# Moving the score maxima and the v maxima between partitions by DMA in a hash-masked attention kernel, with reshaped casts and a new hand-written order

## The chip, the cores and the metric

The kernel runs on one core of a Trainium2 chip. The metric is the device time of one execution in microseconds (us), as the median of several runs. TensorE (PE) multiplies matrices, VectorE (DVE), ScalarE (ACT) and GpSimd (POOL) work on tiles, and SyncE (SP) issues the DMAs of this kernel.

## The reference

Three stages follow each other: an attention whose mask comes from hash buckets, and two feed-forward layers. Cut to what matters:

```python
q_bits = (einsum('bhsd,dk->bhsk', q, proj) > 0)      # 6 bits for each query, the same for keys
mask = q_bucket[:, :, :, None] == k_bucket[:, :, None, :]
scores = where(mask, scale * q @ k.T, -1e9)          # B, H, S, D = 2, 8, 768, 64
attn = exp(scores - scores.max(-1)); attn = attn / (attn.sum(-1) + 1e-9)
x = (attn @ v) as [1536, 512]
h = x @ w_in;  g = P(h) / (Q(h) + 1e-6);  x = g @ w_out     # 512 -> 2048 -> 512
h = x @ w_in2; g = h - tanh(h);           out = g @ w_out2
```

## The kernel before, in words

The attention works on 16 heads, one after another in a software pipeline. Each head has 768 queries and 768 keys, cut into six blocks of 128 (`j`). For a head, in this order:

- `load_qk` loads k and q as one tile with 128 partitions, `split_hi` (ACT) and `split_lo` (POOL) make a rounded part and a rest, and `place` copies them by six DMAs into the operands `TAk`, `TAq`, `TBk`, `TBq`.
- `bits` makes the hash bits with six matmuls. Its out part (DVE) writes them into rows 64 to 107 of `TBk`, and a DMA takes the rows of q into `TBq`.
- `smax` (L456) multiplies a block of 128 queries, taken as weights, by all keys, and DVE takes the maximum of each query over the keys (L460). That is one number in each partition, six columns to a head (`mx`).
- `put_max`, `put_half` (L471 to L477) bring these maxima into row 76 of `TBq`: TensorE transposes `mx` into PSUM (`mt`), DVE negates and bounds it (`mr`), a DMA copies it into the row. There it takes part in the second matmul of `scores`.
- `scores` (L582) makes the transposed scores of a block of keys, ACT takes the exponential (L585). `round_e` rounds it to 16 bits (`eh`), a part on ACT (L591) and the rest on DVE (L593), split by `EH_ACT`; `rest_e` makes the rest `el` on POOL (L602), in the last head partly on DVE (L600).
- `attend` (L634 to L637) multiplies blocks of `eh` and `el` as weights by v in two halves, 18 matmuls of 64 or 65 columns for each `j`; `normalize` divides (DVE).

For each pair of heads v is loaded, and a scale, the same for all partitions, is found from the largest absolute value of each head. `vmax` (L499, DVE) takes a maximum in each partition; `vall` transposes it on TensorE (L508); the `vback` part (L512, L513, DVE) reduces it; the `vagain` part (L516, TensorE) spreads it over the partitions by two small matmuls; `vscale` (L526 to L529, DVE) makes the scale `vsc`. `vhi` (L548, ACT) and `vlo` (L557, DVE; for heads 0 and 1 ACT and POOL) split v into two 16-bit halves, `vmean_of` (L564) adds up v by matmuls. `mt`, `vt` and `vm` share one PSUM bank, the pool `sgl` with one buffer. `fill` (L615) issues matmuls whose result nobody reads. From head 9 on, weights of the first layer are prepared as well (L173 on ACT, L187 and L192 on DVE, L199 on ACT, L200 on POOL). At the end of the attention four blocks of the first layer (`hr`) are woven in with the last head.

The order on every engine is written out by hand: each step has a place in units of one `j`, six to a head, in the tables `T`, `EARLY`, `T_LAST`, and `on(place, step)` sorts them. Engines run their instructions in that order. SP too takes its DMAs in order. The two layers have places in a second table, corrected by `NUDGE`.

Of the kernel before, what the change touches and what calls it, by code (L numbers as in the profile page):

```python
# [10 lines left out]
F32, F32R, F16, I32 = DT.float32, DT.float32r, DT.float16, DT.int32  # L11
# [22 lines left out]
M = dict(a=1, b=3.35, c=3.69, d=5, e=5, y=1.59, scale=3.71, join=3.82, halves=6.35)  # L34
# [10 lines left out]
T = dict(load=-21.57, hi=-15.42, lo=-15.12, place=-14.05, place_a=-12.96, bits=-13.55, bits_out=-12.65,  # L45
         put=-3.12, put_out=-3.08, vhi=-8.38, vlo=-3.99, vmean=-1.97, vmean_out=-0.81, lead=9.98, max=0.3,
         exp=0.42, round=0.9, rest=1.38, pv=(5.37, 6.95, 7.8, 8.75, 8.44, 9.16), pv_last=(5.41, 6.77, 8.07,
         9.01, 8.75, 8.94), norm=9.81, x=14.6, x_out=15.27, v=-16.72, vmax=-11.72, vall=-10.45, vscale=-9.9,
         h0=0.72, slot=0.93, a=0.84, b=1.9, c=2.24, d=4.03, e=4.17, gates=24.8, vback=-10.25, vagain=-9.92,
         w_load=6.0, wt=(-41.29, -22.72, -17.84, -12.24, -8.26, -4.0, 0.32, 3.85), ls=1.0)  # L50
EARLY = {0: dict(load=-61.69, hi=-62.14, lo=-60.39, place=-60.58, bits=-58.96, bits_out=-57.68, place_a=-58.4,
                lead=52.54, put=-46.37, v=-63.23, vmax=-58.62, vall=-56.52, vscale=-54.29, vhi=-6.88,
                vlo=-6.75, vmean=-5.12, vmean_out=-2.89, vback=-56.49, vagain=-55.68, put_half=-47.77,
                ls=0.86),
         1: dict(load=-67.13, hi=-65.44, lo=-65.19, place=-64.04, bits=-59.08, bits_out=-58.81, place_a=-57.52,
                lead=54.94, ls=1.12),
         2: dict(load=-64.89, hi=-61.91, lo=-61.61, place=-61.57, place_a=-61.53, bits=-58.68, bits_out=-58.14,
                lead=9.66, v=-20.61, ls=1.03),
         3: dict(load=-22.52, hi=-15.52, lo=-14.68, place=-14.44, place_a=-13.73, bits=-12.32, bits_out=-11.43,
                lead=9.64)}  # L60
NE = 1
T_LAST = dict(norm=9.87, x=10.11, x_out=10.68)
# [17 lines left out]
 'x_lo 1 1 1': 7.93,  # L80
# [5 lines left out]
 't_sum 1 5 0 3': -0.73}  # L86
# [36 lines left out]
def tile_fn(ctx: ExitStack, tc: tile.TileContext, kq, v, proj, w1i, w1o, a_, b_, w2i, w2o, out):  # L123
# [197 lines left out]
    with ExitStack() as actx:  # L321
# [5 lines left out]

        def single(name):
            return sgl.tile([P, 512], F32, name=name, tag="s")
# [121 lines left out]
        def smax(h, j):  # L451
            if j == 0:
                mx[h] = ap.tile([P, NK], F32, name=f"mx{h}", tag="mx", bufs=4)
            ps = double(f"sm{h}_{j}")[:, :, 0:SH]
            for n in range(2):
                nc.tensor.matmul(ps[:, n], TBq[h][0:76, j * P:(j + 1) * P],  # L456
                                 TBk[h][0:76, n * SH:(n + 1) * SH], start=True, stop=True)

            def out():
                d = nc.vector.tensor_reduce(mx[h][:, j:j + 1], ps, axis=AX.XY, op=ALU.max)  # L460
                if j == NK - 1:
                    sent.setdefault("max", d.ins)

            outs["max", (h, j)] = out
# [37 lines left out]
        nc.vector.memset(pj, 1.0)  # L502
        ones2 = pj[0:2]

        def vall(pr):

            ps = single(f"vt{pr}")
            nc.tensor.transpose(ps[0:2, 0:P], vmx.pop(pr), ident)  # L508

            def back():  # L510
                m = ps[0:2, P + 8:P + 9]
                nc.vector.tensor_reduce(m, ps[0:2, 0:P], axis=AX.X, op=ALU.max)  # L512
                nc.vector.tensor_mul(dg, ident[0:2, 0:2], m.to_broadcast([2, 2]))  # L513

            def again():
                nc.tensor.matmul(ps[:, P:P + 2], ones2, dg, start=True, stop=True)  # L516
                vmx[pr] = ps[:, P:P + 2]

            dg = ap.tile([2, 2], F32, name=f"vdg{pr}", tag="vdg", bufs=2)
            outs["vback", pr], outs["vagain", pr] = back, again  # L520

        def vscale(pr):

            x = vmx.pop(pr)
            xi = x.bitcast(I32)
# [19 lines left out]
        EPS = 1024.0 * 1e-9  # L545
# [14 lines left out]
        def vmean_of(h):  # L560
            ps = single(f"vm{h}")[:, 0:D]
# [5 lines left out]
            def out():  # L567
                t, c = VM[h % 3], 2.0 ** 14 * EPS / S
# [18 lines left out]
        def round_e(h, j):  # L587
            eh[h, j] = ap.tile([P, S], F16, name=f"eh{h}_{j}", tag="eh", bufs=6)
            n = (EH_ACT if h < BH - 1 else EH_ACT_LAST)[j]
            if n:  # L590
                nc.scalar.copy(eh[h, j][:, 0:n], ef[h, j][:, 0:n])  # L591
            if n < S:
                nc.vector.tensor_copy(eh[h, j][:, n:S], ef[h, j][:, n:S])  # L593

        def rest_e(h, j):
            el[h, j] = ap.tile([P, S], F16, name=f"el{h}_{j}", tag="el", bufs=6)
            n = (EL_DVE if h < BH - 1 else EL_DVE_LAST)[j]
            e = ef.pop((h, j))
# [8 lines left out]
        def fill(n):  # L607

            if not warm:
                warm.append(pvp.tile([P, 512], F32, name=f"pvw{len(pv)}", tag="pv"))  # L610
                new = True
            else:
                new = False
            for x in range(n):
                nc.tensor.matmul(warm[0][:, NK * PW:512], ones16, ones16[:, 0:512 - NK * PW], start=new and x == 0,  # L615
                                 stop=False, skip_group_check=True)

        def attend(h, j):
# [13 lines left out]
            for t in range(NK):  # L632
                q = slice(t * P, (t + 1) * P)
                nc.tensor.matmul(out(t), a[:, q], vb[:, j, 0:PW], start=False, stop=False, skip_group_check=True)  # L634
                nc.tensor.matmul(out(t)[:, 0:D], a[:, q], vb[:, j, PW:PW + D], start=False, stop=False,  # L635
# [56 lines left out]
        for h in range(BH):  # L692
# [30 lines left out]
            if h % 2 == 0:  # L723
# [5 lines left out]
                on(g + T["vscale"], vscale, h // 2)  # L729
# [18 lines left out]
        on(TT["gates"] + 2, out_of, "gates", 0)  # L748
        for _, _, fn, args in sorted(tasks, key=lambda x: x[:2]):
            fn(*args)  # L750

# [428 lines left out]
```

## Time and profile before

| | |
|---|---|
| median of 3 runs | 766.49 us (766.38 to 767.56) |
| the profiled execution's own time | 770.33 us |
| its span, first to last instruction | 768.5 us |
| attention, to the first large matmul of the layers | 0 to 260 us of the span |
| first layer, second layer | 260 to about 503, about 503 to 764 us |
| TensorE busy | 740.6 us (96% of the span) |

Times of rows are microseconds from the start of the span. A busy TensorE is not TensorE at its peak, since matmuls overlap: the start of one to the start of the next is its real price. [...]

### The profile page before, as it was taken

The numbers are of one execution on the slowest core, as the hardware profiler recorded it, in microseconds if no ns is written. First come the engines' busy times: TensorE is split into PE (matmuls) and PEld (weight loads), VectorE is DVE, ScalarE is ACT, GpSimd is POOL, SyncE is SP. The second block draws the span as 40 slices with busy tenths as digits, with TensorE's granted clock in tenths as the row PEclk, the third lists the DMA queues.
The fourth block names the chain that finished last, engine by engine and source line by source line (L and its number), as shares of the span: only waits on it lengthen the run. The fifth ranks groups of instructions, "written<-read, shape, count | busy, mean of one in ns | idle before, by whom it ended". The sixth has DMA issues, their size and how long they took to land.

```text
span 768.5 us, 13965 instructions
## 1 busy us (share of the span) xinstructions
PE 740.6 (96%) x5273; PEld 639.6 (83%) x5273; DVE 625.3 (81%) x988; ACT 492.6 (64%) x831; POOL 556.4 (72%) x458
## 2 busy tenths in 40 slices
PE   5999999999998899999999999999999999999997
PEld 3888888888786788888888888887989899989886
DVE  6688999999988888879899998999656766767655
ACT  2577888878896788776666677767554354344421
POOL 3498999898998687787777789968555465465621
PEclk9699999999999999999999999999999999999999
DMA  7573546537421231121121212201031220311003
GB/s 195 147 181 108 146 130 166 158 93 191 119 85 55 71 95 56 55 82 56 57 81 56 82 29 64 73 1 56 27 110 41 70 82 28 110 55 55 28 28 137
DMA packets 41051, 66.52 MB, mean 87 GB/s; under 512 B 3844, under 2 KB 27492, under 8 KB 40984
## 3 DMA queue, kind: packets, MB, share of 16 engines
q1 hardware_dynamic: 40984, 65.63, 29.4%
q8 instruction: 41, 0.67, 0.4%
q14 instruction: 26, 0.21, 0.1%
HBM read 43.00 MB, written 3.15 MB: 60 GB/s over the span
## 4 chain that ended last, share of the span: by engine, by line
PE 77%; DVE 12%; POOL 4%; issue 2%; ACT 2%; DMA 1%; SPq 0%; ACTq 0%; DVEq 0%; POOLq 0%
PE y L1005 17%; PE y L784 12%; PE h L262 12%; PE st L582 7%; PE h2b L922 6%; PE h2e L922 4%; PE h2a L922 4%; PE sm L456 3%; DVE mx L460 3%; PE bits L431 2%; PE hr L262 2%; PE pv L634 1%; PE pv L635 1%; DVE eh L593 1%; PE pv L637 1%
## 5 line engine op out<-in xcount | busy, mean ns | idle before, releaser
L602 POOL TENSOR_TENSOR el<-e,eh 128x768 f16<-128x768 f32 (+1 forms) x95 | 158.8, 1687 | 26.1 <-ACT eh L591 15.1
L1005 PE MATMUL y<-wO,G 128*128 128x512 f32 x576 | 145.1, 393 | 0.3 <-POOL G L990 0.3
L990 POOL TENSOR_TENSOR G<-tmp,G 128x384 fp32r<-128x384 f32 x64 | 66.1, 1034 | 95.6 <-ACT G L985 85.6
L1005 PEld LDWEIGHTS y<-wO,G 128*128 128x128 f32 x576 | 107.0, 188 | 19.1 <-POOL G L990 0.8
L585 ACT ACTIVATE e<-st,lnk 128x768 f32<-128x768 f32 x96 | 86.2, 899 | 29.8 <-PE st L582 26.6
L460 DVE TENSOR_REDUCE mx<-sm 128x1 f32<-128x768 f32 x96 | 90.2, 951 | 9.6 <-PE sm L456 8.4
L1020 DVE TENSOR_TENSOR ya<-y,ya 128x512 f32<-128x512 f32 x84 | 58.1, 692 | 34.5 <-PE y L1005 34.5
L318 POOL TENSOR_TENSOR G<-vec,G 128x512 fp32r<-128x512 f32 x44 | 57.1, 1304 | 26.1 <-ACT G L313 26.0
L591 ACT CAST eh<-e 128x768 f16<-128x768 f32 (+2 forms) x93 | 65.8, 708 | 1.9
L784 PE MATMUL y<-G,wO 128*128 128x512 f32 x288 | 66.7, 389 | 0.0
L784 PE MATMUL y<-G,wE 128*128 128x512 f32 x288 | 66.3, 389 | 0.0
L262 PE MATMUL h<-x,wO 128*128 128x512 f32 x288 | 66.3, 389 | 0.0
L582 PE MATMUL st<-TA 128*128 128x384 f32 x192 | 57.5, 381 | 6.3 <-DVE wt L192 3.3
L784 PEld LDWEIGHTS y<-G,wE 128*128 128x128 f32 x288 | 54.1, 188 | 11.2
L262 PEld LDWEIGHTS h<-x,wO 128*128 128x128 f32 x288 | 54.1, 188 | 11.2
L784 PEld LDWEIGHTS y<-G,wO 128*128 128x128 f32 x288 | 54.0, 188 | 11.1
L634 PEld LDWEIGHTS <-eh 128*128 128x128 f16 x576 | 53.4, 97 | 9.2 <-issue 8.7
L634 PE MATMUL pv<-VB,eh 128*128 128x65 f16 x540 | 59.5, 195 | 0.0
L635 PE MATMUL pv<-VB,eh 128*128 128x64 f16 x540 | 59.1, 196 | 0.0
L637 PE MATMUL pv<-VB,el 128*128 128x65 f16 x540 | 58.6, 193 | 0.4 <-POOL el L602 0.4
L922 PE MATMUL h2b<-x,wE 128*128 128x384 f32 x288 | 58.1, 336 | 0.6 <-DVE tmp L938 0.6
L456 PE MATMUL sm<-TBk,TBq 76*128 76x384 f32 x192 | 54.7, 372 | 3.4 <-DVE mx L460 2.0
(170 smaller groups left out, 1877.4 us busy)
## 6 DMA issues: line engine op xcount, KB each, us to landing
raw<-in_w1i_dram SPq DMA_DIRECT2D x16, 512.0 KB
raw<-in_w1o_dram SPq DMA_DIRECT2D x16, 512.0 KB
raw<-in_w2i_dram SPq DMA_DIRECT2D x16, 512.0 KB
raw<-in_w2o_dram SPq DMA_DIRECT2D x16, 512.0 KB
kq<-in_kq_dram SPq DMA_DIRECT2D x16, 384.0 KB
TA<-A SPq DMA_DIRECT2D x32, 192.0 KB
TA<-Bl SPq DMA_DIRECT2D x32, 192.0 KB
vraw<-in_v_dram SPq DMA_DIRECT2D x8, 384.0 KB
```

Of the source, the lines that this page charges most:

```text
L262: nc.tensor.matmul(ps, l[:, dc], r, start=(n == 0), stop=(n == 11))
L456: nc.tensor.matmul(ps[:, n], TBq[h][0:76, j * P:(j + 1) * P], TBk[h][0:76, n * SH:(n + 1) * SH], start=True, stop=True)
L460: d = nc.vector.tensor_reduce(mx[h][:, j:j + 1], ps, axis=AX.XY, op=ALU.max)
L582: nc.tensor.matmul(ps[:, n], l[h][0:k, j * P:(j + 1) * P], q[h][0:k, n * SH:(n + 1) * SH], start=(k == P), stop=(k < P))
L585: outs["e", (h, j)] = lambda: nc.scalar.activation(halved(e), ps, AF.Exp, scale=1.0 / math.sqrt(D), bias=lnk)
L602: nc.gpsimd.tensor_sub(el[h, j][:, n:S], e[:, n:S], eh[h, j][:, n:S])
L634: nc.tensor.matmul(out(t), a[:, q], vb[:, j, 0:PW], start=False, stop=False, skip_group_check=True)
L635: nc.tensor.matmul(out(t)[:, 0:D], a[:, q], vb[:, j, PW:PW + D], start=False, stop=False, skip_group_check=True)
L637: nc.tensor.matmul(out(t), l[:, q], vb[:, j, 0:PW], start=False, stop=(j == NK - 1), skip_group_check=True)
L784: nc.tensor.matmul(ps, l[:, o], r, start=(n == 0), stop=(n == 11))
L922: nc.tensor.matmul(banks[n, k], w_in(j, l)[:, o:o + P], x[:, r, dt], start=new and z == 0, stop=z == 5, skip_group_check=not new)
L1005: nc.tensor.matmul(ps, g[:, l, o], r, start=(z == 0), stop=(z == 5))
```

## The change

Score maxima: block `j` of `smax` now takes every sixth query, `6 p + j`, as its 128 weights. So partition `p` holds six neighbouring queries, DVE negates and bounds `mx` where it lies, and one DMA from 128 partitions (24 bytes each) writes row 76. The transpose goes. v maxima: a DMA brings `vmx` into one partition, DVE reduces it and makes the scale there, a second DMA spreads the scale over 128 partitions; the transposes, the small matmuls and `vscale` go. Casts: the DVE part of `eh` has 3 or 5 rows of 128 (before, 256 or 640 columns in one run), in rows of 130 places. `vlo`: ACT writes the scaled v into PSUM, DVE subtracts from there. One PSUM bank, `sbank`, is kept for the sums of v, the scaled v and the scale. In `vback` three more instructions, those of `vscale`, run on the one partition. Fillers, places and nudges are new; a `fill` that opens a new PSUM tile after the first `vmean_of` issues a quarter as many matmuls of 512 columns. A program `before` looks over the order while the kernel is built; it adds no instruction.

```diff
-EH_ACT = (768, 768, 128, 768, 512, 768)
+EH_ACT = (384, 768, 128, 768, 384, 768)
+EP = P + 2
-EH_ACT_LAST = (0, 0, 768, 0, 640, 768)
-EL_DVE_LAST = (128, 0, 0, 128, 128, 768)
-FILL = ((1.54, 30), (100.1, 16), (200, 50))
+EH_ACT_LAST = (128, 0, 768, 384, 768, 768)
+EL_DVE_LAST = (640, 0, 0, 640, 640, 768)
+FILL = ((100.1, 31), (199.95, 71), (-62.62, 25), (-57.32, 46), (-1.76, 12), (91.54, 25))
...
         def smax(h, j):
-                nc.tensor.matmul(ps[:, n], TBq[h][0:76, j * P:(j + 1) * P],
+                nc.tensor.matmul(ps[:, n], TBq[h][0:76].rearrange("k (p t) -> k t p", p=P)[:, j],
                                  TBk[h][0:76, n * SH:(n + 1) * SH], start=True, stop=True)
...
         def put_part(h, m, t0, n):
-            ps = single(f"mt{h}_{t0}")[0:n, 0:P]
-            nc.tensor.transpose(ps, m[:, t0:t0 + n], ident)
+            mr = ap.tile([P, n], F32R, name=f"mr{h}_{t0}", tag="mr", bufs=2)
...
+            nc.vector.tensor_scalar(mr, m, -1.0, -LOWEST, op0=ALU.mult, op1=ALU.min)
             def out():
-                mr = ap.tile([n, P], F32R, name=f"mr{h}_{t0}", tag="mr", bufs=2)
-                nc.vector.tensor_scalar(mr, ps, -1.0, -LOWEST, op0=ALU.mult, op1=ALU.min)
-                nc.sync.dma_start(TBq[h][76:77, t0 * P:(t0 + n) * P].bitcast(F32), mr.bitcast(F32))
+                row = TBq[h][76:77].bitcast(F32).rearrange("o (p t) -> o p t", p=P)
+                src = mr.bitcast(F32)
+                nc.sync.dma_start(row[:, :, t0:t0 + n], src if n < NK else src.rearrange("p a b -> p (a b)"))
...
         def vall(pr):
-            ps = single(f"vt{pr}")
-            nc.tensor.transpose(ps[0:2, 0:P], vmx.pop(pr), ident)
+            row = ap.tile([1, 2 * P], F32, name=f"vrow{pr}", tag="vrow", bufs=2)
+            nc.sync.dma_start(row.rearrange("o (p h) -> o p h", h=2), vmx.pop(pr))
+            sc = ap.tile([1, 2], F32, name=f"vs1{pr}", tag="vs1", bufs=2)
             def back():
-                m = ps[0:2, P + 8:P + 9]
-                nc.vector.tensor_reduce(m, ps[0:2, 0:P], axis=AX.X, op=ALU.max)
-                nc.vector.tensor_mul(dg, ident[0:2, 0:2], m.to_broadcast([2, 2]))
+                o = SH + D + 2 * (pr % 2)
+                x = sbank[0:1, o:o + 2]
+                nc.vector.tensor_reduce(x, row.rearrange("o (p h) -> o h p", h=2), axis=AX.X, op=ALU.max)
...
             def again():
-                nc.tensor.matmul(ps[:, P:P + 2], ones2, dg, start=True, stop=True)
+                vs = ap.tile([P, 2], F32, name=f"vsc{pr}", tag="vsc", bufs=3)
+                nc.sync.dma_start(vs, sc.unsqueeze(1).to_broadcast([1, P, 2]))
...
         def vlo(h):
-            nc.vector.scalar_tensor_tensor(out=t[:, :, D + 1:2 * D + 1], in0=vsl(h), scalar=vsc[h],
-                                           in1=t[:, :, 0:D], op0=ALU.mult, op1=ALU.subtract)
+            x = sbank[:, 0:SH].rearrange("p (t d) -> p t d", t=NK)
+            nc.scalar.activation(x, vsl(h), AF.Copy, scale=vsc[h])
+            nc.vector.tensor_sub(t[:, :, D + 1:2 * D + 1], x, t[:, :, 0:D])
...
         def round_e(h, j):
-            eh[h, j] = ap.tile([P, S], F16, name=f"eh{h}_{j}", tag="eh", bufs=6)
+            t = ap.tile([P, NK * EP], F16, name=f"eh{h}_{j}", tag="eh", bufs=6)
+            w = P if n == S else EP
+            t = eh[h, j] = t[:, 0:NK * w].rearrange("p (t w) -> p t w", w=w)[:, :, 0:P]
+            r, e = n // P, ef[h, j].rearrange("p (t w) -> p t w", w=P)
...
         def fill(n):
...
+            if new and VM_SET:
+                w = VB[0][:, 0:4, 0:P]
+                for x in range(n // 4):
+                    nc.tensor.matmul(warm[0].rearrange("p (a b) -> p a b", a=4), ones16, w, start=x == 0, stop=False,
+                                     skip_group_check=True)
+                return
```

Of the places, those of the steps that move data between partitions are, before and after: `put` -3.12 and -3.09, `vmax` -11.72 and -12.75, `vall` -10.45 and -12.36, `vback` -10.25 and -10.26, `vagain` -9.92 and -9.9, `vhi` -8.38 and -7.56, `vlo` -3.99 and -4.8, `place` -14.05 and -13.78, `bits_out` -12.65 and -12.91. In the first pair `vall` and `vback` stand together at -56.59.

## Rows read from the trace of the kernel before

**Rows 1.** Busy time of each engine, granted clock and DMA: two heads, then the layers' joint.

```profile
79.09:91.55 12.46, 12.46 (x173) 11.39 (x173) 11.34 (x22) 10.64 (x18) 11.20 (x7) 1.00 0.47 117
...
157.50:171.98 14.48, 13.42 (x179) 11.71 (x176) 14.08 (x24) 10.20 (x16) 13.08 (x9) 1.00 0.45 114
...
500.00:510.00 10.00, 8.57 (x43) 7.47 (x43) 9.62 (x19) 5.74 (x12) 3.91 (x4) 1.00 0.01 2
```

**Rows 2.** The chain that ended last, in order of time: start, duration, what.

```profile
26.75 2.72 PE st L582 x8
29.48 2.88 PE pvw L615 x30
...
79.09 1.12 PE bits L431 x6
...
143.29 1.11 PE bits L431 x6
...
238.65 3.63 PE hr L262 x12
```

**Rows 3.** Groups of VectorE by shape, 40 to 240 us: busy, mean ns, idle before.

```profile
L593 DVE CAST eh<-e 128x256 f16<-128x256 f32 x14 | 18.7, 1338 | 0.1
...
L557 DVE SCALAR_TENSOR_TENSOR VB<-vraw,vsc,VB 128x384 f16<-128x384 f32 x14 | 12.8, 916 | 0.2
L593 DVE CAST eh<-e 128x640 f16<-128x640 f32 x14 | 12.4, 889 | 1.0 <-ACT e L585 1.0
L651 DVE TENSOR_TENSOR xt<-pv,rz 128x384 f32<-128x384 f32 x14 | 7.8, 557 | 0.5
```

**Rows 4.** VectorE in order of time, at 92 us.

```profile
92.24 1.83 DVE L593 CAST eh<-e 128x256 f16<-128x256 f32 x1
```

**Rows 5.** GpSimd in order of time, at 90 us.

```profile
90.64 3.28 POOL L602 TENSOR_TENSOR el<-e,eh 128x768 f16<-128x768 f32 x2
```

**Rows 6.** Stretches at the start and the end of the attention, columns as in rows 1.

```profile
20.00:32.00 12.00, 11.70 (x64) 9.89 (x63) 8.04 (x12) 4.43 (x7) 1.64 (x1) 0.50 0.78 202
...
235.00:238.40 3.40, 2.95 (x31) 2.61 (x32) 3.30 (x8) 2.61 (x4) 3.40 (x3) 0.77 0.44 154
```

**Rows 7.** TensorE in order of time, 86 to 95 us.

```profile
86.26 0.51 PE L456 MATMUL sm<-TBk,TBq 76*128 76x384 f32 x2
...
87.00 0.20 PE L634 MATMUL pv<-VB,eh 128*128 128x65 f16 x1
...
88.13 0.27 PE L471 MATMUL mt<-ident,mx 128*6 128x128 f32 x1
...
88.59 0.52 PE L582 MATMUL st<-TBq,TBk 77*128 77x384 f32 x2
88.94 0.52 PE L456 MATMUL sm<-TBk,TBq 76*128 76x384 f32 x2
...
94.88 0.52 PE L582 MATMUL st<-TBq,TBk 77*128 77x384 f32 x2
```

**Rows 8.** Single lines: ns least, median and most; first and last start; shapes.

```profile
L499 DVE TENSOR_REDUCE vm<-vraw x8: 947/953/955, 6.6 to 189.9; 128x2 f32<-128x768 f32 x8
...
L508 PEld LDWEIGHTS vt<-ident,vm x8: 80/82/122, 7.7 to 191.1; 128*2 128x2 f32 x8
...
L456 PEld LDWEIGHTS sm<-TBk,TBq x192: 186/189/338, 13.1 to 218.4; 76*128 76x128 f32 x192
```

**Rows 9.** Groups of ScalarE by shape, 40 to 240 us, columns as in rows 3.

```profile
L591 ACT CAST eh<-e 128x768 f16<-128x768 f32 x59 | 48.9, 828 | 1.3
...
L591 ACT CAST eh<-e 128x512 f16<-128x512 f32 x14 | 8.7, 619 | 0.4
L548 ACT ACTIVATE VB<-vraw,vsc 128x384 f16<-128x384 f32 x13 | 8.0, 615 | 0.0
```

**Rows 10.** SP's DMA issues in order of time, at 89 us.

```profile
89.20 0.78 SPq L477 DMA_DIRECT2D TBq<-mr  x1
```

**Rows 11.** The chain at 176 us, a DMA between partitions.

```profile
176.30 3.18 DMA TBq<-TBk
```

More of the change, by code (lines that the diff above doesn't have):

```diff
@@ L40 @@
+EH_ACT_LAST = (128, 0, 768, 384, 768, 768)
+EL_DVE_LAST = (640, 0, 0, 640, 640, 768)
+FILL = ((100.1, 31), (199.95, 71), (-62.62, 25), (-57.32, 46), (-1.76, 12), (91.54, 25))
 VLO_POOL = (0, 1)
 EL_DVE = (0, 0, 0, 0, 0, 0)
[L45 to L60, printed above, removed]
+T = {'load': -22.33,
+ 'hi': -18.56,
+ 'lo': -16.18,
+ 'place': -13.78,
+ 'place_a': -13.04,
+ 'bits': -13.52,
+ 'bits_out': -12.91,
+ 'put': -3.09,
+ 'put_out': -3.08,
+ 'vhi': -7.56,
+ 'vlo': -4.8,
+ 'vmean': -2.43,
+ 'vmean_out': -1.12,
+ 'lead': 9.85,
+ 'max': 0.3,
+ 'exp': 0.42,
+ 'round': 0.95,
+ 'rest': 1.36,
+ 'pv': (5.37, 6.95, 6.95, 8.46, 7.97, 9.54),
+ 'pv_last': (5.41, 6.4, 8.07, 9.01, 8.9, 9.11),
+ 'norm': 9.78,
+ 'x': 14.6,
+ 'x_out': 15.0,
+ 'v': -16.72,
+ 'vmax': -12.75,
+ 'vall': -12.36,
+ 'h0': 0.65,
+ 'slot': 0.93,
+ 'a': 0.8,
+ 'b': 1.89,
+ 'c': 2.29,
+ 'd': 4.03,
+ 'e': 4.46,
+ 'gates': 22.24,
+ 'vback': -10.26,
+ 'vagain': -9.9,
+ 'w_load': 6.42,
+ 'wt': (-41.29, -21.14, -17.84, -12.15, -6.33, -4.04, 0.32, 3.85),
+ 'ls': 0.98}
@@ new lines @@
+EARLY = {0: {'load': -61.72,
+     'hi': -61.84,
+     'lo': -60.39,
+     'place': -60.59,
+     'bits': -58.99,
+     'bits_out': -56.82,
+     'place_a': -58.76,
+     'lead': 51.69,
+     'put': -46.8,
+     'v': -63.23,
+     'vmax': -58.82,
+     'vall': -56.59,
+     'vhi': -6.83,
+     'vlo': -6.75,
+     'vmean': -4.75,
+     'vmean_out': -2.89,
+     'vback': -56.59,
+     'vagain': -55.68,
+     'put_half': -47.77,
+     'ls': 0.87,
+     'x': 14.71},
+ 1: {'load': -66.87,
+     'hi': -66.39,
+     'lo': -65.13,
+     'place': -64.04,
+     'bits': -59.08,
+     'bits_out': -58.62,
+     'place_a': -57.5,
+     'lead': 52.34,
+     'ls': 1.45,
+     'vagain': -10.08,
+     'vlo': -3.71},
+ 2: {'load': -65.08,
+     'hi': -61.83,
+     'lo': -61.61,
+     'place': -61.6,
+     'place_a': -61.53,
+     'bits': -59.14,
+     'bits_out': -58.14,
+     'lead': 9.91,
+     'v': -20.19,
+     'ls': 1.16},
+ 3: {'load': -22.14,
+     'hi': -15.52,
+     'lo': -14.72,
+     'place': -15.44,
+     'place_a': -12.68,
+     'bits': -12.26,
+     'bits_out': -11.25,
+     'lead': 9.62,
+     'ls': 1.0}}
@@ L567, in out @@
             def out():
+                still(f"vm{h}")
                 t, c = VM[h % 3], 2.0 ** 14 * EPS / S
@@ L748, in tile_fn, with before @@
         on(TT["gates"] + 2, out_of, "gates", 0)
-        for _, _, fn, args in sorted(tasks, key=lambda x: x[:2]):
+        def before(what, h=None, j=None):
+            out = lambda w, k=h: ("out_of", w, k)
+            every = range(NK)
+            return {
+                "split_lo": [("split_hi", h)], "place": [("split_hi", h)], "bits": [("split_lo", h)],
+                "place out": [("place", h), ("split_lo", h)], "bits out": [("bits", h)],
+                "smax": [out("bits"), ("place", h)],
+                "put_max": [out("max", (h, x)) for x in every],
+                "put_half": [out("max", (0, x)) for x in every[h or 0:(h or 0) + NK // 2]],
+                "scores": [out("place"), out("bits")] + ([out("put")] if h else [("put_half", 0), ("put_half", 3)]),
+                "round_e": [out("e", (h, j))], "rest_e": [("round_e", h, j)],
+                "attend": [("rest_e", h, j), ("vlo", h), out("vmean")]
+                + ([("attend", h, 0)] if j else []),
+                "vhi": [("out_of", "vagain", (h or 0) // 2)] + [("attend", h - 3, x) for x in every if h and h > 2],
+                "vlo": [("vhi", h)], "vmean_of": [("vlo", h)],
+                "vmean out": [("attend", h - 3, 0)] if h and h > 2 else [],
+                "normalize": [("attend", h, x) for x in every] + ([("normalize", h - 1)] if h else []),
+                "to_x": [("normalize", 2 * h + 1)] if h is not None else [],
+                "vall": [("vmax", h)], "vback out": [("vall", h)], "vagain out": [out("vback")],
+                "stage_a": [("out_of", "gates", 0)],
+                "h_mm": [out("x", x) for x in range(4)],
+            }.get(what, [])
+        done = set()
+        for _, _, fn, args in sorted(tasks, key=lambda x: x[:2]):
+            name = fn.__name__
+            what = (args[0] + " out", args[1]) if name == "out_of" else (name, *args)
+            if not isinstance(what[1] if len(what) > 1 else 0, tuple):
+                missing = [x for x in before(*what[:3]) if x not in done]
+                assert not missing, (what, missing)
             fn(*args)
+            done.add((name, *args))
     mp = ctx.enter_context(tc.tile_pool(name="mp", bufs=1, reuse_waits="tile"))
```

81 lines of the change are left out of this document (47 added, 34 removed).

## The prediction

> **What bounds the kernel.** I read first the windows by engine. In the layers TensorE has no gaps but at their joint, where 8.57 of 10 us are busy [rows 1]; the rest runs at one steady pace, and the diff changes no instruction there. So the change can win or lose almost only in the attention, the first 260 us. There the same view is to be read by head. At 79 us a head takes 12.46 us, and TensorE is busy for all of it; VectorE has 11.34 of the 12.46. At 157 us a head takes 14.48 us, and now VectorE is the full one with 14.08, while TensorE has 13.42 [rows 1]. The chain that ended last gives the mean of many heads from the starts of `bits`: from 79.09 to 143.29 us there are five heads of 12.84 us, from 143.29 to 238.65 us seven of 13.62 us [rows 2]. So there are three places with different limits: a start of some 40 us, heads that TensorE paces, and late heads, in which weights are prepared too, that VectorE paces.
>
> The next view is VectorE's groups by shape. A cast of 256 columns takes 1338 ns on average, one of 640 columns 889 ns, so the smaller one takes longer; and `vlo` takes 916 ns for 384 columns, where a subtraction of 384 columns that reads PSUM takes 557 ns [rows 3]. In order of time one sees why: a 256-column cast starts at 92.24 us and takes 1.83 us, to 94.07 [rows 4], and GpSimd's pair of `el` runs from 90.64 to 93.92 us [rows 5]. The cast ends 0.15 us after GpSimd is done: it waited for it. A reduction that reads one tile of SBUF never waits: 947 to 955 ns for all eight [rows 8].
>
> [...]
>
> **The change part by part.** The sum is made against the profiled execution's 770.33 us (the span of 768.5 and 1.8 around it); I take the same difference off the median, 766.49.
>
> *TensorE's instructions.* The transpose `mt` starts at 88.13 us, two matmuls of `st` follow it, and the next two start at 88.59. Two such matmuls take 0.35 us (88.59 to 88.94), so `mt` costs 0.11 us [rows 7]; the v transpose has the same form. The two small matmuls of `vagain` stand between an `sm` pair that starts at 86.26 and ends its turn 0.35 us later, and a `pv` at 87.00: 0.39 us with their wait [rows 7]. A pair of heads loses 2 x 0.11 + 0.11 + 0.39 = 0.72 us. In eight heads from 40 to 143 us, where TensorE paces, that is 4 x 0.72 = 2.9 us. The bounds are 0 (another engine is next at once) and 8 x 0.72 = 5.8 (all heads).
>
> *Casts and `vlo`.* If the new casts behave as a single-source instruction that never waits, their price follows from 953 ns for 768 columns [rows 8] and 557 for 384 [rows 3]: 1.03 ns a column, so 0.56 us for 384 and 0.82 for 640. A head then has 0.56 + 0.82 + 0.56 = 1.94 us where it had 1.34 + 0.89 = 2.23. `vlo` as a subtraction that reads PSUM goes from 0.92 to 0.56. Together 0.65 us of VectorE's time a head. The other bound: the casts still wait, three of about 1.1 us, and a head gains 1.0 us of casts. Rows show waits only for the forms that run faster than one column a nanosecond or read two tiles of SBUF, so I take the first. [...]
>
> On the late heads VectorE sets the pace. They cost 13.62 - 12.84 = 0.78 us more than the earlier ones [rows 2]. I let them lose half of that, 0.39, and half of the 0.72 us of a pair, 0.36: 7 x 0.75 = 5.2 us. Bounds: 0, and the whole 0.78 + 0.36, 8.0.
>
> *ScalarE.* A head's casts go from four of 768, one of 512 and one of 128 columns to three of 768, one of 128 and two of 384. It loses 0.83 + 0.62 [rows 9], gains two of about 0.51 (between the shapes by columns) and `vlo`'s scaling, 0.62, the price of the same scaling in `vhi` [rows 9]: +0.19 us on 10.64 of 12.46 [rows 1]. It is covered by ScalarE's idle time, 1.8 us a head; where a head is compressed that cover gets thin. `el` on GpSimd is unchanged, two in 3.28 us [rows 5], so six in 9.8 and with `split_lo` about 12 of a head. GpSimd is therefore close behind TensorE: I take off 1 us for this in all.
>
> *New DMAs.* The maxima: the DMA was issued at 89.20 us [rows 10], and the first matmul of `st` that reads row 76 starts at 94.88 [rows 7], a budget of 5.7 us. The nearest row for its duration, a DMA between partitions that the chain waited for, is 3.18 us [rows 11]. The new one has more and smaller pieces. Bounds 3.2 (hidden) and above 5.7 (each head waits). I take hidden. For v two DMAs replace two steps on TensorE. From `vall` to `vback` there are 2.1 places, and from `vagain` to `vhi` 2.3, at 2.1 us each: 4.4 and 4.9 us against 3.2. But VectorE runs in order: if the first is late, the maxima of `sm` queued behind `vback` wait, and TensorE for their banks; if the second is late, `vhi` holds up the exponentials behind it on ScalarE. In the start `vback` stands directly behind `vall` and surely waits, about 3 us, in a time when VectorE waits for TensorE anyway. I take 8 x 0.25 = 2 us.
>
> *Start.* The filler of 30 matmuls takes 2.88 us of the chain [rows 2]. It goes; 12 others stay in front of the scores, 0.6 us at full clock, since 2.88 / 30 is 0.096 at half clock. The eight matmuls of `st` in front of it take 2.72 us; at full clock 4 x 0.35 = 1.4 [rows 2, 7]. New fillers stand from the first microseconds on, so I expect the clock to be up from there; before about 20 us VectorE paces and nothing is won. 2.3 + 1.3 = 3.6; less the wait for `vback` I take 3.0, bounds -1 and 6.
>
> *End of the attention and joint.* The stretch at 0.77 [rows 6] and the `hr` block of 3.63 us, which at full pace takes some 2.8 [rows 2], cost about 1.5 us; the new filler in the last head stands there. I take 1.5. The moves at the layers' joint get 0.5 of the 1.43 us idle [rows 1], bounds 0 and 1.4. More fillers at 100.1 and 199.95 run in a wait for VectorE and cost nothing; without that cover some 1 us.
>
> Sum: 2.9 + 5.2 + 3.0 + 1.5 + 0.5 - 1.0 - 2.0 = 10.1 us, so 770.33 becomes 760.2, and the median 756.4.
>
> **The rivals.** *Weights in strides (the other side).* `smax` now takes its 128 weights from places 24 bytes apart; every load in this trace reads neighbours. A load of 2 columns takes 82 ns, one of 128 columns 189 ns [rows 8], so the columns cost 0.85 ns each, 107 ns, and they hide behind a matmul of 0.175 us [rows 7]. At half rate the load needs 214 ns and each of 192 matmuls [rows 8] is 0.04 us longer: 7.7 us, for a time of 764. At a quarter rate it needs 428: 192 x 0.25 = 48 us, 805. The time before is reached at 10.1 / 192 = 0.053 us more a matmul, a load of some 0.23 us. For it speaks only that the stride is new; against it that the load has room. [...] I give 0.24 to half rate and 0.06 to worse.
>
> *DMAs in place of TensorE's steps are late.* If each pair waits 1.5 us at `vback` or `vhi` and the last two maxima are late, 8 x 1.5 = 12 us instead of 2 are lost: 766.5. The rows' 3.18 us speak against it, the queue in front (six DMAs of `place` in each head) for it. Chance 0.13.
>
> *The next engine takes over.* If GpSimd or ScalarE holds the middle heads at today's pace, and the casts still wait, only the start, the end and half of the late heads remain: 3.0 + 2.0 + 2.6 - 2 = 5.6, about 761. Chance 0.12.
>
> **How the numbers follow.** The forecast has 0.45. Its own range by the bounds of its terms is 748 to 763. Half-rate loads and the takeover lie in 761 to 766, late DMAs around 766. Leaving out the worse loads and the tails, 747 to 770 holds 8 in 10. A measurement of this kernel can tell about 0.2%, 1.5 us, from no change. Faster: 0.45 + 0.21 of the loads + 0.03 of the late DMAs + 0.10 of the takeover, less a little for the forecast's own tail: 0.76. Same: 0.07. Slower: 0.17, from worse loads, late DMAs and a few half-rate cases.
>
> **What would show it.** Right: `sm` weight loads of 189 ns again, casts of 0.56 and 0.82 us with least and most close together, no PE wait for `vsc`, a granted clock near 1.00 from 20 to 32 us, heads of about 12.5 us up to the middle and 12.9 after. Wrong: loads of `sm` above 230 ns and `sm` pairs further apart than 0.35 us; VectorE idle on a DMA in front of the reduction of `vback`; `vhi` released by a DMA; `st` waiting for row 76; heads still near 12.8 with GpSimd without gaps.

## The result, and the profile after

The changed kernel takes 760.20 us (median of four runs, 758.95 to 761.26); beside it the kernel before took 766.62. The ratio is 0.9913, with an interval of 0.9892 to 0.9934: 0.9% faster. The forecast was 756.4, its range 747 to 770. The profiled execution of before (770.33) lies 3.7 us above the median of its runs and that of after is the shortest of its four, so the two traces differ by 11.4 us where the medians differ by 6.4; where a gain is read from one pair of stretches, this stands behind it.

The windows of the kernel after (columns as in [rows 1]): the head of the first row there and its neighbour, the head of the second row and its neighbour, the joint, which now comes 11 us earlier, and the start:

```profile
77.09:89.59 12.50, 12.50 (x169) 11.97 (x169) 12.07 (x22) 10.92 (x19) 10.17 (x7) 1.00 0.48 115
89.59:102.61 13.02, 13.02 (x175) 12.55 (x175) 10.77 (x17) 11.51 (x19) 12.65 (x9) 1.00 0.61 172
...
154.01:166.41 12.40, 12.40 (x169) 11.91 (x169) 12.04 (x22) 10.73 (x17) 10.82 (x8) 1.00 0.48 115
166.41:179.43 13.02, 13.02 (x175) 12.55 (x175) 10.77 (x17) 11.51 (x19) 12.58 (x9) 1.00 0.70 203
488.60:498.60 10.00, 8.75 (x45) 7.65 (x44) 9.62 (x19) 5.74 (x12) 3.98 (x4) 1.00 0.01 2
...
20.00:32.00 12.00, 11.64 (x49) 8.69 (x49) 10.73 (x15) 2.58 (x5) 2.67 (x2) 0.50 0.90 227
```

TensorE is now without a gap in these heads, and the late ones take as long as the middle ones, 12.40 and 13.02 us in turn (two others take 13.57 and 13.16). The price of a head in the middle has hardly moved, 12.50 and 13.02 us in turn where the mean was 12.84 [rows 2]. From 20 to 32 us the granted clock is 0.50, half of full speed, as before [rows 6].

Lines of the chain that ended last (start, duration, what), to set beside [rows 2]:

```profile
11.39 3.80 DMA vrow<-vm
...
77.25 1.04 PE bits L524 x6
...
140.61 1.04 PE bits L524 x6
...
229.48 5.55 PE hr L348 x24
```

So the start is 1.84 us shorter (79.09 to 77.25, forecast 3.0), the five middle heads 0.84 (64.20 to 63.36; by the forecast 5/8 of 2.9, 1.8), the late heads 6.5 (95.36 to 88.87; forecast 5.2 and part of the end's 1.5), and from the first block of `hr` to the end of the span 2.1 (529.85 to 527.72). Of that, the joint has 0.18: its idle time was 1.43 us and is 1.25, where the forecast took 0.5 off.

The 1.84 us of the start are not firm. In the profiled execution of before one head was slow, with the granted clock at 0.89 in the mean. The same head in a run of the kernel before that differs only in strided weights (below, `b1_strided`) took 2.3 us less:

```profile
49.62:65.11 15.49, 14.12 (x173) 12.76 (x173) 13.18 (x20) 10.72 (x16) 12.19 (x8) 0.89 0.43 106
...
50.09:63.32 13.23, 13.09 (x174) 12.31 (x173) 12.15 (x20) 10.43 (x16) 10.96 (x8) 1.00 0.43 109
```

The forecast's other steps can be checked in the groups of the attention (line, engine, operation, shapes, count; busy us, mean ns; idle before):

```profile
L551 PEld LDWEIGHTS sm<-TBk,TBq 76*128 76x128 f32 x192 | 51.5, 316 | 8.5 <-DVE TBk L534 4.4 <-DVE mx L555 3.7 <-ACT e L675 0.2
L686 DVE CAST eh<-e 128x384 f16<-128x384 f32 x31 | 17.1, 551 | 1.6 <-ACT e L675 0.9
L686 DVE CAST eh<-e 128x640 f16<-128x640 f32 x16 | 12.9, 808 | 1.6 <-ACT e L675 1.5
L646 DVE TENSOR_TENSOR VB<-sbank,VB 128x384 f16<-128x384 f32 x14 | 7.7, 553 | 1.7 <-ACT sbank L645 1.7
```

The casts take 0.55 and 0.81 us, `vlo` 0.55: as reckoned. The first row is the one that was to show the forecast wrong: a load of `sm`'s weights takes 316 ns on average, over all 192, where half of them took no more than 189 [rows 8]. That is the rival of weights in strides.

### The profile page after: what moved, and what is told of

The parts are those of the page before. It is cut to its first block, busy times and chain, and to the rows that moved or that the text cites. A ratio compares the mean times of both kernels' runs of the same rounds, so it can differ in the third digit from the quotient of the medians.

```text
span 757.2 us, 14111 instructions
## 1 busy us (share of the span) xinstructions
PE 740.8 (98%) x5322; PEld 652.2 (86%) x5322; DVE 613.7 (81%) x993; ACT 493.4 (65%) x847; POOL 545.2 (72%) x458
## 4 chain that ended last, share of the span: by engine, by line
PE 83%; DVE 7%; POOL 4%; DMA 2%; issue 1%; ACT 1%; SPq 0%; DVEq 0%; ACTq 0%; POOLq 0%
PE y L1134 17%; PE y L913 13%; PE h L348 12%; PE st L672 9%; PE h2b L1051 6%; PE sm L551 5%; PE h2e L1051 4%; PE h2a L1051 4%; PE pv L733 2%; PE pv L734 2%; PE pv L736 2%; PE bits L524 2%; PE hr L348 1%; POOL G L404 1%; DVE mx L555 1%
## 5 line engine op out<-in xcount | busy, mean ns | idle before, releaser
L695 POOL TENSOR_TENSOR el<-e,eh 128x768 f16<-128x768 f32 (+1 forms) x95 | 150.9, 1609 | 24.8 <-DVE eh L686 10.4
L551 PE MATMUL sm<-TBk,TBq 76*128 76x384 f32 x192 | 62.9, 417 | 4.8 <-DVE TBk L534 3.7
L684 ACT CAST eh<-e 128x384 f16<-128x384 f32 (+2 forms) x95 | 60.4, 636 | 1.9
L551 PEld LDWEIGHTS sm<-TBk,TBq 76*128 76x128 f32 x192 | 51.5, 316 | 8.5 <-DVE TBk L534 4.4
L733 PE MATMUL pv<-VB,eh 128*128 128x65 f16 x540 | 57.7, 194 | 0.0
L734 PE MATMUL pv<-VB,eh 128*128 128x64 f16 x540 | 57.2, 195 | 0.0
```

The costliest lines, as they stand in the source:

```text
L551: nc.tensor.matmul(ps[:, n], TBq[h][0:76].rearrange("k (p t) -> k t p", p=P)[:, j], TBk[h][0:76, n * SH:(n + 1) * SH], start=True, stop=True)
L695: nc.gpsimd.tensor_sub(l[:, r:NK], e[:, r:NK], eh[h, j][:, r:NK])
L733: nc.tensor.matmul(out(t), a[:, t], vb[:, j, 0:PW], start=False, stop=False, skip_group_check=True)
L734: nc.tensor.matmul(out(t)[:, 0:D], a[:, t], vb[:, j, PW:PW + D], start=False, stop=False, skip_group_check=True)
```

## The experiments

Ratios are to the kernel before, run on the same chip, with their intervals. The unaltered changed kernel ran once more as the yardstick.

> The changed kernel unaltered, on the chip of the next three, to compare them with. Between 758.5 and 761.5 us, as in the runs shown, 5 to 8 us under the kernel before.

It took 760.02 us, ratio 0.9883 (0.9869 to 0.9898). Differences below are taken from it. The yardstick ran together with the first three edits of the changed kernel (weights, casts, v). The others ran at other times, beside a kernel before of their own. For them the ratio counts as much as the microseconds, and a difference of 2 or 3 us is not shown by the times alone: the unaltered changed kernel had a ratio of 0.9913 first and of 0.9883 here, 2.3 us apart.

**The strided weights, both ways.** In the changed kernel the stride goes; in the kernel before it comes:

```diff
# changed kernel, a1_next_to
-                nc.tensor.matmul(ps[:, n], TBq[h][0:76].rearrange("k (p t) -> k t p", p=P)[:, j],
+                nc.tensor.matmul(ps[:, n], TBq[h][0:76, j * P:(j + 1) * P],
# kernel before, b1_strided
-                nc.tensor.matmul(ps[:, n], TBq[h][0:76, j * P:(j + 1) * P],
+                nc.tensor.matmul(ps[:, n], TBq[h][0:76].rearrange("k (p t) -> k t p", p=P)[:, j],
```

> The changed kernel with weights of neighbouring queries in smax again, nothing else altered; the maxima then reach other queries' places in row 76, so only its time counts. Theory (strided weights load at half rate, and this is paid where TensorE paces): sm loads fall from 316 to 189 ns, an sm pair takes 0.35 us where it took 0.45, a middle head goes from 12.7 to about 12.2 us, the time falls by 5 to 9 us, to 751 to 755. Rival (GpSimd or ScalarE takes over at once): the loads fall as well, but the heads stay at 12.5 or more, and the time falls by less than 3 us.

> The kernel before with weights of every sixth query in smax and nothing else altered; its transposes still stand, so maxima reach other queries' places in row 76. Theory (loads at half rate, 0.04 to 0.05 us a matmul where TensorE paces): loads of 0.32 us, sm pairs of 0.45 us, 4 to 8 us slower than the kernel before. Rival (in the kernel before VectorE's and GpSimd's waits leave room): less than 2 us slower, though the loads are as long.

Without the stride the changed kernel takes 752.64 us, ratio 0.9792 (0.9776 to 0.9809): 7.4 us less. With it the kernel before takes 774.29, ratio 1.0089 (1.0063 to 1.0115), 8.2 more than the 766.07 beside it. In both, row 76 then holds the maxima of other queries, so only the times count. The lines of the loads and of their matmuls (ns least, median and most; first and last start), first without the stride in the changed kernel:

```profile
L551 PEld LDWEIGHTS sm<-TBk,TBq x192: 186/189/338, 12.7 to 204.6; 76*128 76x128 f32 x192
...
L551 PE MATMUL sm<-TBk,TBq x192: 331/338/690, 12.9 to 204.8; 76*128 76x384 f32 x192
```

and with it in the kernel before:

```profile
L456 PEld LDWEIGHTS sm<-TBk,TBq x192: 296/318/333, 12.7 to 222.2; 76*128 76x128 f32 x192
...
L456 PE MATMUL sm<-TBk,TBq x192: 381/392/698, 13.0 to 222.4; 76*128 76x384 f32 x192
```

These matmuls take 383, 392 and 700 ns in the changed kernel as it is, and 331, 338 and 688 in the kernel before as it was. In either kernel the load goes from 189 to some 320 ns and its matmul from 338 to 392. 54 ns by 192 are 10.4 us of engine time, of which 7.4 and 8.2 reach the end. The price is one of the stride, not of the new order around it. Where it falls fits the prediction's picture of heads with different limits: in the kernel before the five heads that TensorE paces go from 64.2 to 68.8 us in these two traces, the late ones, which VectorE paces, from 95.3 to 95.9. What in a load of strided weights takes longer is not shown; these runs give its size for places 24 bytes apart.

**The casts with odd rows.**

```diff
-EP = P + 2
+EP = P
```

> The changed kernel with the casts' rows at a pitch of 128 places, so that three or five rows are one run of columns again. Theory (the odd rows end the casts' waits for GpSimd): casts of 384 columns spread between 0.35 and 2 us and take about 1.1 us on average where they took 0.55, VectorE gets some 1 us a head more, and the late heads slow down by half of that: 3 to 6 us slower than the changed kernel, 763 to 766. Rival (the casts' gain is hidden, TensorE paces in nearly all heads now): less than 1.5 us slower.

764.37 us, ratio 0.9944 (0.9929 to 0.9959), 4.35 slower. The line of the casts, first in the changed kernel, then in this run:

```profile
L686 DVE CAST eh<-e x48: 542/554/821, 33.3 to 227.9; 128x384 f16<-128x384 f32 x31, 128x640 f16<-128x640 f32 x16, 128x768 f16<-128x768 f32 x1
...
L686 DVE CAST eh<-e x48: 348/660/1830, 32.3 to 233.5; 128x384 f16<-128x384 f32 x31, 128x640 f16<-128x640 f32 x16, 128x768 f16<-128x768 f32 x1
```

The quickest cast is now 348 ns, quicker than any with odd rows (542 to 821 in the changed kernel), and the median is slower, 660 against 554, as is the longest, 1830 against 821. So with the two places of padding no cast is as quick, and none stands longer than its shape takes: the spread of 542 to 821 ns is that of the shapes, 0.54 to 0.56 us for 384 columns and 0.80 to 0.82 for 640. In the trace of before, in one run of columns, the casts of 640 columns take from 0.48 to 1.94 us, the quickest 0.75 ns a column. That is the reading of [rows 3, 4, 5], and it is worth 4.35 us. By which property of the rows a cast is of the one kind or the other is not shown.

**v through PSUM.** `vlo` is one VectorE instruction again, which reads v and the rounded half from SBUF:

```diff
-            x = sbank[:, 0:SH].rearrange("p (t d) -> p t d", t=NK)
-            nc.scalar.activation(x, vsl(h), AF.Copy, scale=vsc[h])
-            nc.vector.tensor_sub(t[:, :, D + 1:2 * D + 1], x, t[:, :, 0:D])
+            nc.vector.scalar_tensor_tensor(out=t[:, :, D + 1:2 * D + 1], in0=vsl(h), scalar=vsc[h],
+                                           in1=t[:, :, 0:D], op0=ALU.mult, op1=ALU.subtract)
```

> The changed kernel with vlo as one instruction of VectorE that reads two tiles of SBUF, as before; ScalarE's scaling into PSUM goes. Theory (v through PSUM ends a wait for GpSimd): the instruction takes 0.9 us on average with a spread of 0.6 to 2 us where it took 0.55, and the time is 1 to 3 us longer, 761 to 763. Rival (ScalarE's 0.6 us a head costs as much as VectorE's wait): within 1 us, or shorter.

770.73 us, ratio 1.0012 (0.9988 to 1.0037): 10.7 slower in the median, more than the whole gain of the change, but not all of it is the instruction's own. The extra does not come in small parts. The line of `vlo`, then VectorE in order of time:

```profile
L644 DVE SCALAR_TENSOR_TENSOR VB<-vraw,vsc,VB x14: 608/640/5084, 46.0 to 218.9; 128x384 f16<-128x384 f32 x14
...
45.98 5.08 DVE L644 SCALAR_TENSOR_TENSOR VB<-vraw,vsc,VB 128x384 f16<-128x384 f32 x1
50.99 1.81 DVE L555 TENSOR_REDUCE mx<-sm 128x1 f32<-128x768 f32 x2
```

and GpSimd in order of time, and the windows, in the same kernel:

```profile
39.33 7.93 POOL L694 TENSOR_TENSOR el<-e,eh 128x768 f16<-128x768 f32 x5
47.23 1.83 POOL L499 TENSOR_TENSOR Bl<-kq,A 128x768 fp32r<-128x768 f32 x1
49.02 1.63 POOL L694 TENSOR_TENSOR el<-e,eh 128x768 f16<-128x768 f32 x1
...
48.00:52.00 4.00, 0.71 (x20) 0.59 (x19) 4.00 (x3) 0.96 (x2) 2.65 (x2) 0.90 0.13 50
52.00:56.00 4.00, 4.00 (x37) 3.69 (x38) 3.15 (x7) 1.73 (x2) 1.96 (x2) 0.50 0.34 85
```

Half of the `vlo` take 0.64 us or less. One stands from 45.98 to 51.06 while GpSimd works from 39.33 to 50.65 without a gap, and ends 0.41 us behind it, through several instructions of GpSimd. The maxima queue behind it, TensorE runs dry (0.71 of 4 us) and comes back at half clock (0.50 from 52 to 56 us). Against the yardstick this head takes 16.2 us from `bits` to `bits` instead of 10.4: 5.8 of the 12.3 us between the two traces are this one event. Another 3.3 stand at the first large matmul of the layers, which waits 3.24 us for VectorE's `g`, and 1.7 behind it, where its first 48 matmuls take 12.80 us instead of 11.06. No `vlo` stands there, and why that wait comes with this edit is not shown. In the other heads together it is under 1 us. The event does not seem to fall in every execution: three of the ten took 764.10 to 766.91 us, the other seven 770.71 to 772.63, some 5 us more.

**TensorE brings the score maxima again.** As before the change, a transpose into the shared bank, and neighbouring weights with it:

```diff
-            mr = ap.tile([P, n], F32R, name=f"mr{h}_{t0}", tag="mr", bufs=2)
...
-            nc.vector.tensor_scalar(mr, m, -1.0, -LOWEST, op0=ALU.mult, op1=ALU.min)
+            ps = sbank[0:n, 0:P]
+            nc.tensor.transpose(ps, m[:, t0:t0 + n], ident)
             def out():
+                mr = ap.tile([n, P], F32R, name=f"mr{h}_{t0}", tag="mr", bufs=2)
+                nc.vector.tensor_scalar(mr, ps, -1.0, -LOWEST, op0=ALU.mult, op1=ALU.min)
+                nc.sync.dma_start(TBq[h][76:77, t0 * P:(t0 + n) * P].bitcast(F32), mr.bitcast(F32))
```

> The changed kernel with the score maxima on TensorE's transpose again (neighbouring queries as weights, transpose into sbank, VectorE from PSUM, six long pieces by DMA); v's maxima stay with the DMA. Theory (strides cost 7.4 us, transposes 0.11 us each): 752.6 plus 17 x 0.11 = 1.9, so 753 to 756. Rival (the transpose and VectorE's longer step bring waits on the shared PSUM bank back): 757 to 761.

758.10 us, ratio 0.9876 (0.9844 to 0.9907): by the medians 1.9 us less than the yardstick, by the ratios 0.5, which is not clear of nothing. It is 5.5 us more than without the stride and without the transpose. The waits of 40 to 230 us (engine, line, what it waited for: us, times, longest):

```profile
DVE mr L566 <- PE sbank L562: 2.7, 7, 0.4
...
PEld sbank L562 <- DVE vs L604: 2.1, 4, 0.6
```

Neither wait exists in the changed kernel. The transpose comes back with a queue: it shares its bank with the v scale.

But not all of the 5.5 us belongs to the transposes. In the last head an `el` on VectorE takes 3.70 us in this trace, and 2.08 in that of a run further down that has the same order there (`a6_pe_max_late`). VectorE and GpSimd, first here, then there:

```profile
218.38 3.70 DVE L687 TENSOR_TENSOR el<-e,eh 128x640 f16<-128x640 f32 x1
...
211.80 8.36 POOL L689 TENSOR_TENSOR el<-e,eh 128x768 f16<-128x768 f32 x6
220.12 1.27 POOL L286 TENSOR_TENSOR wE<-wt,wE 128x512 fp32r<-128x512 f32 x1
...
218.65 2.08 DVE L687 TENSOR_TENSOR el<-e,eh 128x640 f16<-128x640 f32 x1
...
212.06 8.95 POOL L689 TENSOR_TENSOR el<-e,eh 128x768 f16<-128x768 f32 x6
```

Here the `el` ends 0.69 us behind GpSimd's chain. There it ends 0.28 us before the chain does, and the chain takes longer, 8.95 us for 8.36. From the last `bits` to the first `hr` it is 38.65 us here and 36.25 there, so the wait costs 2.4. The changed kernel can have it too: without its first fillers the same `el` took 3.81 us, in the yardstick 2.16. The four executions here took 757.97 to 758.89 us and, one of them, 755.22.

The heads before that are a better measure. From the `bits` of head 3 to those of the last head it is 145.8 us without stride and transpose, 149.3 and 149.0 with transposes, and 151.3 in the yardstick. In these twelve heads the transposes that the change took out are worth 3.2 to 3.5 us, and the strides that it took in for them cost 5.5.

**Neighbouring weights and six DMAs.** A DMA for each column of maxima keeps the weights side by side without a transpose:

```diff
-                nc.sync.dma_start(row[:, :, t0:t0 + n], src if n < NK else src.rearrange("p a b -> p (a b)"))
+                for t in range(n):
+                    nc.sync.dma_start(TBq[h][76:77, (t0 + t) * P:(t0 + t + 1) * P].bitcast(F32), src[:, t:t + 1])
```

> The weights of the score maxima lie next to each other again, and the maxima still go to row 76 by DMA, now by one DMA for each of the six columns (three for a half of the first head): 128 pieces of 4 bytes each instead of 128 pieces of 24 bytes. All of the computation is kept. If only the stride of the loads cost time and the DMAs stay hidden, this comes out where the variant with neighbouring weights did, at 751.5 to 754. Rival: an issue of such a DMA takes 0.5 us on SyncE's queue, so the last of six is issued 3.0 us after the negated maxima are there and leaves some 3.2 us for it to land; the copies of the next head behind it come 2.5 us later. If either is late, each middle head loses some 0.5 us or more, and the time is 758 to 766.

785.35 us, ratio 1.0223 (1.0202 to 1.0244): worse than either expectation. All issues of the maxima (ns least, median and most), SyncE in order of time, then VectorE two microseconds earlier:

```profile
L574 SPq DMA_DIRECT2D TBq<-mr x96: 492/599/1780, 25.1 to 241.7; - x96
...
92.88 0.51 SPq L601 DMA_DIRECT2D vrow<-vm  x1
...
98.69 4.72 SPq L574 DMA_DIRECT2D TBq<-mr  x6
103.51 0.53 SPq L507 DMA_DIRECT2D TBk<-A  x1
...
96.75 0.42 DVE L607 TENSOR_REDUCE sbank<-vrow 1x2 f32<-1x256 f32 x1 [1.28 <-DMA vrow<-vm]
```

An issue takes 0.6 us in the median, not the 0.5 reckoned. Six in a row take 3.7 us and more (4.72 here, where one of them took 1.6), so everything behind the maxima is 3 to 4 us late, the v maxima too. VectorE now waits for `vrow` in four pairs, 5.1 us in all, with the maxima of `sm` behind it: the late-DMA rival's first step, as it was written. The whole loss is far larger than that rival's, 32.7 us against the same weights with one DMA. The longest head takes 18.1 us, where it was 13.3, and the granted clock of the span is 0.967 instead of 0.990; which late DMA starts which of these waits was not traced. In the changed kernel itself no wait of VectorE for that DMA stands after 45 us.

**The start.** `vback` of the first pair later, behind the first maxima:

```diff
-     'vback': -56.59,
-     'vagain': -55.68,
+     'vback': -49.2,
+     'vagain': -49.1,
```

> The changed kernel with vback and vagain of the first pair moved behind the hash bits of head 1 (from -56.59 and -55.68 to -49.2 and -49.1). Theory (the 4.9 us that VectorE stands idle for the first vrow holds up the hash bits of head 1 and all that follows): bits of head 1 leave VectorE by 14 us where it was 17.3, TensorE's gap before 17.4 us is gone, the clock does not fall to half there, and the time falls by 2 to 5 us. Rival (the start waits for the loads and copies by DMA anyway, or the scores wait for the second half of head 0's maxima): less than 1 us.

> Both edits, transposes for the score maxima and the later vback. If they are independent, the two gains add up: 749 to 754 us. If the start is bound elsewhere, as the transposes alone.

> The same, and in the first pair the reduction of the v maxima is taken later, as in the earlier run with only that change, which won 1.2 us. If both hold as before, 750 to 753; if the start is held by the longer queue of copies on SyncE, no better than the variant with six DMAs alone, within 1 us of it.

Alone it gives 758.85 us, ratio 0.9893 (0.9872 to 0.9914): 1.2 us less than the yardstick, but no better by the ratio, so no gain is shown. With TensorE's maxima 755.25, ratio 0.9849 (0.9829 to 0.987): the best version whose maxima reach their own places. It is 1.5% faster than the kernel before, and by the ratios 2.6 us faster than the yardstick, with intervals that just touch. The trace says where: a pair of its heads takes 12.46 and 12.58 us instead of 12.41 and 13.02, with loads of 189 ns again. The later `vback` has no share in it that can be seen: the `bits` of head 3 start at 40.80 us, without it at 40.21, and the rest of the difference to the transposes alone is the wait of `el` shown above. With six DMAs 782.33, ratio 1.019 (1.0161 to 1.0219). VectorE, then ScalarE, of the run with this edit alone:

```profile
12.75 1.09 DVE L534 TENSOR_SCALAR TBk<-bits,thr,amp 44x768 fp32r<-44x768 f32 x1 [2.69 <-PE bits L524]
...
26.77 0.61 ACT L635 ACTIVATE VB<-vraw,vsc 128x384 f16<-128x384 f32 x1 [7.61 <-DMA vsc<-vs]
```

The hash bits leave VectorE 3.5 us earlier (at 13.84, not 17.32), but then `vhi` waits for the scale, whose DMA comes behind six copies that SyncE issues from 19.2 to 22.9 us; the first scores start at 30.64 us (30.71 in the kernel after). The wait moved, and the rival was right.

**The fillers.** Those of the first 11 us, and the one of the last head, which is 25 matmuls of 122 columns, and not, as the expectation has it, six of 512:

```diff
# c1_no_start_fill
-FILL = ((100.1, 31), (199.95, 71), (-62.62, 25), (-57.32, 46), (-1.76, 12), (91.54, 25))
+FILL = ((100.1, 31), (199.95, 71), (-1.76, 12), (91.54, 25))
# c2_no_last_fill
+FILL = ((100.1, 31), (199.95, 71), (-62.62, 25), (-57.32, 46), (-1.76, 12))
```

> The changed kernel without the two fillers of its first 11 us, 25 and 46 matmuls whose result nobody reads. The prediction counted on them for a clock at full speed from 20 to 32 us and gave the start 3.0 us. My theory now: they won nothing there, since the granted clock is 0.50 from 16 to 32 us with them as it was without them, and TensorE waits for the v maxima behind them; the time stays within 1.5 us of the changed kernel's, 758.5 to 761.5. Rival: without them the hash bits and the first maxima run at half clock earlier, the maxima of the first head come later, and the time is 2 us or more longer, above 762.

> The changed kernel without the filler in the last head, six matmuls of 512 columns. The prediction put the 1.5 us of the attention's end down to it. By that the time is 1 to 2 us longer, 761 to 762, with a granted clock below 1.00 where the first blocks of the first layer begin. Rival: the other order of the last head, with its rests on VectorE in larger parts, brought the gain, and the filler brings less than 0.7 us: 759.3 to 760.7, with the clock at 1.00 there all the same.

759.62 us, ratio 0.9897 (0.9862 to 0.9933), and 760.41, ratio 0.9911 (0.989 to 0.9931): neither filler can be told from nothing. (Without the first two the filler in front of the scores changes form as well, three matmuls of 512 columns for 12 of 122.) Without the first two, TensorE from 8 us and the windows:

```profile
8.53 1.01 PE L524 MATMUL bits<-A,pj_hi 128*128 128x384 f32 x2 [1.04 <-ACT A L495]
9.34 0.84 PE L524 MATMUL bits<-A,pj_lo 128*128 128x384 f32 x2
...
20.00:28.00 8.00, 7.67 (x20) 5.02 (x18) 7.87 (x10) 1.46 (x3) 2.67 (x2) 1.00 0.99 227
```

With them the pair at 10.53 us starts 0.43 us before the next, at 10.96; without them the pairs are 0.81 apart. So with the fillers the bits of the second head come at nearly twice the pace, and TensorE then waits 3.7 us for the hash bits anyway. Note the column of the clock: it says 1.00 from 20 to 28 us here, while twelve `sm` matmuls at 23.20 take 5.14 us, as they do at 0.50 in the kernel after (5.13). In this trace the column is 1.00 in all of the first 44 us and does not tell the two paces apart; in such a stretch the distance of like matmuls is to be read. Without the last filler the clock at the end is 1.00 all the same; TensorE only idles 1.14 us for `el` where the filler stood, and from the last `bits` to the first `hr` it is 36.72 us with the filler and without it.

## Why the prediction was right, and where its numbers were not

The direction and the range held; the likeliest case did not happen. What happened is the rival of half-rate weights, with 764 as its time. That 760.2 lies within 4 us of the forecast's 756.4 is in part luck: without the stride the rest of the change earns 2.1%, some 16 us, where the sum had 10.1, so two errors of opposite sign nearly met.

- *The step that failed* is "`sm` weight loads of 189 ns again": the loads were taken as free, since 189 ns had room behind a matmul. Measured 7.4 and 8.2 us; the rival's 7.7 was right, and so was its way. Its load of 214 ns counted the columns alone; with the 82 ns of the two-column load [rows 8] it is 296, the least that was measured, and the median is 318 to 321. Of the 130 ns that the load grew, 54 show on the matmul, and 39 to 43 a matmul in the time.
- *Why the time was 760 and not 764.* Casts and `vlo` were costed together at 0.65 us of VectorE's time a head, and VectorE's relief at 2.7 of the 5.2 us of the late heads. Undone one by one they cost 4.35 and 10.7, the latter with the 5 us at the layers' first matmul that are not explained. The durations were right: that a cast in three or five rows would never wait was the author's estimate, since no trace of before has such a cast, and in the changed kernel none took more than 0.82 us. What was mis-sized is the price of a wait. It was taken as its mean (0.36 us a `vlo`), where the runs show a rare one of 5 us that stops VectorE and TensorE, with a granted clock of 0.50 behind it. (The two numbers need not add up to the gain: each was measured with the other edit in place.)
- *TensorE's instructions*, 2.9 us for eight middle heads, 1.8 for the five measured: these show 0.84. Without the stride they take 60.9 us, 3.3 less than before, so the term was not too high (other parts of the change are in the 3.3 as well); the strides took 2.4 of it.
- *The late heads* gained 6.5 against 5.2 and some of the end's 1.5: right in kind, since in the same head VectorE's 14.08 of 14.48 us became 12.04 of 12.40, and TensorE, now without a gap, paces. Some of it belongs to the execution: with the long wait of `el` in the last head, as without the first fillers, it is 2.5 us less.
- *The start*, 3.0 forecast, 1.84 measured, and most of that is the slow head in the profiled execution of before: with strides put in, the kernel before reaches the same `bits` at 77.43 us, the changed kernel at 77.09, both by the first of these matmuls. "The clock to be up from there" failed: 0.50 from 20 to 32 us. The `vrow` DMA (3.80 us on the chain) holds VectorE 4.92 us, and TensorE behind it 3.70, not in "a time when VectorE waits for TensorE anyway"; later the scale would be late instead. The 12 matmuls in front of the scores, reckoned at 0.6 us, take 1.41 at half clock (0.50).
- *The end*, 1.5: about right in size, wrong in its cause. The filler did nothing. That leaves the other order of the last head, which was not tested by itself. *The joint* gave 0.18 of its 0.5.
- *New DMAs*: hidden in the steady heads, as taken, the 2.0 us held back for them being too much there and too little in the start. The run with six DMAs shows that 3 to 4 us more of queue end this cover.
- *The next engine*: TensorE has no gap, and beside it ScalarE and GpSimd are busy for 11.51 and 12.65 of 13.02 us in the longer head of a pair, 10.92 and 10.17 of 12.50 in the other. That rival's 761 is near the time, but not its reason.

Open: how the 5 us at the layers' first matmul hang together with `vlo` (apart from `vlo` itself, the steps on each engine come in the same order as in the yardstick, by the names of their tiles); what decides in which executions VectorE's instruction ends before GpSimd's chain and in which behind it, since for `el` in the last head both cases occur under the same order; what the new way of the v maxima is worth, since no run undoes it by itself; and whether an order made for a version without strides would keep all of the 752.6 with maxima in their own places.

## What to carry to other kernels

A view that takes an instruction away may hand its cost to an operand: before an access pattern changes from neighbours to strides, ask which engine reads it and whether its loads have room, and test that one line by itself (here a load went from 189 to some 320 ns, which cost 7.4 and 8.2 us). A VectorE instruction that waits for GpSimd can have its price in its rare longest wait and not in its mean (here 5.08 us once, 0.64 in the median): read least, median and most, and what is queued behind it. Before a difference of 2 us is given to an edit, look for such a wait in both traces: here one fell in one execution and not in the other (an `el` of 3.70 us and of 2.08). And count the DMA issues: here VectorE had no wait for the DMA of the v maxima after 45 us, and with 3 to 4 us more of queue it had 5.1 us of them.

## What was not expected of the hardware

Weights 24 bytes apart take 296 to 333 ns a load, 318 to 321 in the median, against 189 in the median for neighbours (186 to 338), and a 384-column matmul behind them 392 against 338 in the median. One VectorE instruction of 0.61 us stood 5.08 us behind GpSimd's unbroken chain, and a 640-column subtraction on VectorE took 3.70 and 3.81 us in two traces and 2.08 and 2.16 in two others, under the same order. A DMA issue of 128 pieces of 4 bytes takes 0.60 us in the median on SyncE's queue (0.49 to 1.78), one of 128 pieces of 24 bytes 0.51 in the median.
